# Attention scores: three rounded passes on the whole array, or plain float32 on its four quarters

## The chip, the cores and the metric

The kernel runs on one core of one Trainium2 chip. The metric is the device time of one execution in microseconds (us), lower is better. TensorE (PE in the profile) multiplies matrices: a stationary operand is loaded into its 128x128 array (PEld), a moving operand streams past it column by column, and the result goes to PSUM, which has eight banks. VectorE (DVE) and ScalarE (ACT) read PSUM; GpSimd (POOL) works on SBUF alone; SyncE (SP) issues the DMAs.

## The reference, cut to what matters

Block-causal attention over 4 x 8 heads of 576 tokens and 64 dimensions, then a squared-ReLU network over all 2304 tokens, then a top-1 mixture of eight experts. The change touches the first stage alone, and in it the scores:

```
scores = scale * matmul(q, k.T)                  # per head: 576 x 576, contraction over 64
scores = where(block_i >= block_j, scores, -1e9) # blocks of 64 tokens
attn = exp(scores - max) / sum
x = matmul(attn, v)
h = x @ w_in; g = s * relu(h)**2 + b; g @ w_out  # 512 -> 2048 -> 512
each token through one of 8 experts, 512 -> 1024 -> 512, chosen by an argmax over logits
```

The argmax over logits makes rounding matter: a token sent to another expert has another output row.

## The kernel before, in words

**Units and blocks.** Two heads of one batch make a unit; there are 16 units of 9 query blocks, so 144 steps. Block `i` of a unit needs the keys 0 to 64(i+1), which is `n` = 64 to 576 columns. Both heads are treated at once: the two transposed heads lie on partitions 0 to 63 and 64 to 127, and a stationary tile of queries is block diagonal (one head's queries in each corner, zeros elsewhere), so that one 128x128 product gives 64 query rows of either head, 128 rows in all.

**Scores (`scores`, L131 to L147).** TensorE multiplies rounded operands (fp32r) in one pass per column, at reduced precision; so queries and keys are split into a high, rounded part and a low rest, and a block takes three products: qh kh, qh kl, ql kh (L144), each over max(n, 256) columns. Blocks 0 and 1, which are narrower than 256, use plain float32 operands `qf`, `kf` (L141); a plain float32 product is two passes, and so stands in the profile as two matmuls. Block 8 has 576 columns and takes two PSUM banks of 288 each. The parts are made per unit by ACT (L104, L107: queries, scaled by 1/8; L119, L120, L128: keys) and DVE (`flush`: L88 and L90, the low parts).

**The rest of a step.** DVE takes the row maxima (L152), ACT the exponentials with their sums (L160), DVE the reciprocals (L177, L178), POOL scales the rows (L169), TensorE transposes them five steps later (L198, plain float32 transposes), ACT copies them out of PSUM (`p_copy`, L211), and `pv` (L227) multiplies them with the values: per head a product of 128 rows and 64 columns of the array in plain float32, the two heads on the two column halves of the array. Queries and keys of the next unit are transposed at blocks 4, 5 and 6 (L95, L125).

**PSUM banks.** The scores have three banks (`s`) in both stages: `BANKS_0 = (3, 3, 1, 1)` and `BANKS_A = (3, 2, 1)`. A bank comes free when the exponentials that read it are done.

**Order.** Up to step 45 (`ORDERED`), which is five units, the order on PE, ACT, DVE and POOL is the order in which the code emits. There the loop over `t` issues, in this order: transposes of step t-5, scores of t, exponentials of t-1, copies, reciprocals of t-2, maxima of t, low parts, a piece of weight conversion, and the next unit's transposes. From step 45 on a planner orders the instructions by the program's order and by its own estimates of when operands and banks are there, and from step 50 on it mixes in pieces of the squared-ReLU network (L470, L545), whose matmuls TensorE does beside attention. What of that network is left follows when attention has ended, near 326 us, and then come the experts. On every engine the instructions then run strictly in the planned order.

Of the kernel before, what the change touches and what calls it, by code (L numbers as in the profile page):

```python
# [9 lines left out]
F32 = mybir.dt.float32  # L10
F32R = mybir.dt.float32r
BF16 = mybir.dt.bfloat16
I32 = mybir.dt.int32
AF = mybir.ActivationFunctionType
ALU = mybir.AluOpType
AX = mybir.AxisListType
PSUM = bass.MemoryType.PSUM
P = 128


def attention(nc, tc, ctx, ps, ident, q, k, v, xT_d, weights):
# [7 lines left out]
    B, H, S, D = q.shape  # L29
    NB = S // D  # L30
    NU = B * H // 2
    pool = lambda n, b, **kw: ctx.enter_context(tc.tile_pool(name=n, bufs=b, **kw))
    fix = pool("a_fix", 1)
    raw = pool("a_raw", 2)
    vp = pool("a_v", 2)
    pt = pool("a_pt", PTBUF)
    kt = pool("a_kt", 2)
    pp = pool("a_p", NPBUF)
# [3 lines left out]
    one = fix.tile([P, 1], F32, name="one")  # L42
    nc.gpsimd.memset(one, 1.0)
    nc.scalar.activation(one, one, AF.Exp)
    qb, qf = [], []
    for par in range(2):
        qq = []
        for nm in ("qh", "ql"):
            t = fix.tile([P, NB - 2, 2, D], F32R, name=f"{nm}{par}")
            nc.gpsimd.memset(t.bitcast(F32), 0.0)  # L50
            qq.append(t)
        qb.append(qq)
        t = fix.tile([P, 2, 2, D], F32, name=f"qf{par}")
        nc.gpsimd.memset(t, 0.0)
        qf.append(t)
    st = {}
    todo = []
    scored = [None]
    copies, sums = [], []

# [17 lines left out]
            ps.last["load"] = nc.sync.dma_start(tail, src[b, h0:h0 + 2, 512:].rearrange("h p d -> p h d"))  # L78
            s["raw"].append(t)

    def low(scale, out, src, high):
        todo.append((scale, out, src, high))

    def flush():
        while todo:
            scale, o, src, high = todo.pop(0)
            if scale:
                nc.vector.scalar_tensor_tensor(o, src, 0.125, high.bitcast(F32), ALU.mult, ALU.subtract)  # L88
            else:
                nc.vector.tensor_sub(o, src, high.bitcast(F32))  # L90

    def transpose4(src):
        t = ps.t.tile([P, 512], F32, name="tw", tag="t")
        for c in range(4):
            nc.tensor.transpose(t[:, c * P:(c + 1) * P], src[:, c].rearrange("p h d -> p (h d)"), ident)  # L95
        return t

    def q_high(u, src, blocks):
        skip = max(2 - blocks.start, 0)
        for hh in range(2):  # L100
            r = slice(hh * D, hh * D + D)
            a = src[r].rearrange("p (i d) -> p i d", d=D)
            if skip:
                nc.scalar.activation(qf[u % 2][r, :, hh], a[:, 0:skip], AF.Copy, scale=0.125)  # L104
                a = a[:, skip:]
            oh, ol = (t[r, blocks.start + skip - 2:blocks.stop - 2, hh] for t in qb[u % 2])
            nc.scalar.activation(oh, a, AF.Copy, scale=0.125)  # L107
            low(True, ol, a, oh)

    def q_transpose(u):  # L110
        q_high(u, transpose4(st[u]["raw"][0]), slice(0, 8))

    def k_transpose(u):
        kh = kt.tile([P, S], F32R, name="kh", tag="kh")
        kl = kt.tile([P, S], F32R, name="kl", tag="kl")
        kf = kt.tile([P, P], F32, name="kf", tag="kf")
        st[u]["k"] = (kh, kl, kf)
        t = transpose4(st[u]["raw"][1])
        nc.scalar.copy(kf, t[:, 0:P])  # L119
        nc.scalar.copy(kh[:, 0:512], t)  # L120
        low(False, kl[:, 0:512], t, kh[:, 0:512])

    def tails(u):
        t = ps.t.tile([P, 512], F32, name="te", tag="t")
        nc.tensor.transpose(t[:, 0:P], st[u]["tail"].rearrange("p h d -> p (h d)"), ident)  # L125
        q_high(u, t[:, 0:D], slice(8, 9))
        kh, kl, _ = st[u]["k"]
        nc.scalar.copy(kh[:, 512:], t[:, D:2 * D])  # L128
        low(False, kl[:, 512:], t[:, D:2 * D], kh[:, 512:])

    def scores(u, i):  # L131
        kh, kl, kf = st[u]["k"]
        qh, ql = qb[u % 2]
        n = (i + 1) * D
        pr = pp.tile([P, 640], F32, name="p", tag="p")
        parts = [(0, n)] if i < 8 else [(0, 288), (288, 288)]
        scs = []
        for k0, w in parts:
            sc = ps.s.tile([P, 512], F32, name="sc", tag="s")
            if i < 2:  # L140
                scored[0] = nc.tensor.matmul(sc[:, 0:w], qf[u % 2][:, i].rearrange("p h d -> p (h d)"),  # L141
                                             kf[:, 0:w], start=True, stop=True)
            for j, (a, kk) in enumerate(((qh, kh), (qh, kl), (ql, kh)) if i >= 2 else ()):
                scored[0] = nc.tensor.matmul(sc[:, 0:max(w, 256)], a[:, i - 2].rearrange("p h d -> p (h d)"),  # L144
                                             kk[:, k0:k0 + max(w, 256)], start=(j == 0), stop=(j == 2))
            scs.append(sc)
        return u, i, pr, parts, scs  # L147

    def maxima(u, i, pr, parts, scs):
        nm = small.tile([P, 2], F32, name="nm", tag="nm")  # L150
# [30 lines left out]
    def p_transpose(u, blocks):  # L181
        i0 = blocks[0]
        grp = int(i0 >= 4)
        if i0 == 4 * grp:
            st[u]["pt", grp] = pt.tile(([P, 4, 2, P], [P, 5, 5, P])[grp], F32, name=f"pt{grp}", tag=f"pt{grp}")
        out = st[u]["pt", grp]
        nch = i0 // 2 + 1
        jobs = []
        if grp == 0:
            jobs.append(([(i, c) for i in blocks for c in range(nch)], out[:, i0:i0 + 2, 0:nch]))  # L190
        else:
            for c0, c1 in ((0, min(4, nch)), (4, nch)):
                if c1 > c0:
                    jobs.append(([(i0, c) for c in range(c0, c1)], out[:, i0 - 4, c0:c1]))
        for lst, o in jobs:
            t = ps.t.tile([P, 512], F32, name="tp", tag="t")
            for e, (i, c) in enumerate(lst):
                nc.tensor.transpose(t[:, e * P:(e + 1) * P], st[u][i][0][:, c * P:(c + 1) * P], ident)  # L198
            src = t[:, 0:len(lst) * P]
            if grp == 0:  # L200
                src = src.rearrange("p (i c n) -> p i c n", i=2, n=P)
            else:
                src = src.rearrange("p (c n) -> p c n", n=P)
            copies.append((i0, o, src))
        for i in blocks:
            st[u].pop(i)

    def p_copy():
        while copies:
            i0, o, src = copies.pop(0)  # L210
            P_COPY(nc, i0)(o, src)  # L211

    def pv(u, grp):

        s = st[u]
        if grp == 0:
            s["x"] = xo.tile([P, S], F32, name="x", tag="x")
        vt, p = s["raw"][2], s.pop(("pt", grp))
        n = 256 if grp == 0 else 320
        o = ps.o.tile([P, 512], F32, name="o", tag="o")  # L220
        cs = range(2) if grp == 0 else range(5)
        with tc.issue_after(scored[0].ins), tc.high_priority():
            for c in cs:
                first = max(0, 2 * c - 4 * grp)
                for hh in range(2):
                    r = slice(hh * D, hh * D + D)
                    nc.tensor.matmul(o[r, first * D:n], vt[:, c, hh], p[:, first:, c, r],  # L227
                                     start=(c == 0), stop=(c == cs[-1]))
        sums.append((u, grp, o, n))

    def x_copy():
# [14 lines left out]
    q_transpose(0)  # L246
    k_transpose(0)
    tails(0)
    flush()
    seq = [(u, i) for u in range(NU) for i in range(NB)]  # L250

    def at(t):
        return seq[t] if 0 <= t < len(seq) else (None, None)
# [24 lines left out]

    done = 0
    maxed = None  # L280
    order = ExitStack()
    order.enter_context(tc.manual_schedule(engines={mybir.EngineType.PE, mybir.EngineType.Activation,
                                                    mybir.EngineType.DVE, mybir.EngineType.Pool}))
    for t in range(len(seq) + LP + 1):
        if t == ORDERED:
            exponentials(*maxed)
            normalise(*at(t - 2))
            order.close()
        u, i = at(t - LP)
        if i in (3, 8):  # L290
            pv(u, int(i == 8))
            done += int(i == 8)
        if t < ORDERED:
            turn(t - LT)
            u, i = at(t)
            now = scores(u, i)
            if t >= 1:
                exponentials(*maxed)
            p_copy()
            x_copy()  # L300
            if t >= 2:
                normalise(*at(t - 2))
            maxed = maxima(*now)
            flush()
            weights(t)
            prepare(u, i)
            loads(u, i)
        else:
            x_copy()
            turn(t - LT)  # L310
            p_copy()
            u, i = at(t)
            if u is not None:
                exponentials(*maxima(*scores(u, i)))
                prepare(u, i)
                loads(u, i)
            u, i = at(t - LN)
            if u is not None:
                normalise(u, i)
            flush()  # L320
            weights(t)
        yield done

# [1160 lines left out]
```

## Time and profile before

| | |
|---|---|
| median of 3 runs | 904.42 us (903.22 to 905.1) |
| the profiled execution, its own time | 904.25 us |
| its span | 902.6 us |
| PE, PEld busy | 875.6 us (97%), 725.2 us (80%) |
| DVE, ACT, POOL busy | 642.5 us (71%), 568.4 us (63%), 215.1 us (24%) |

The page's strip of busy tenths in 40 slices of 22.6 us each:

```profile
PE   7999989999999999999999999999999999999996
PEld 5767777888879789999999999998477776776775
DVE  5898986464646355878967777767688987776783
ACT  6998786566757543333566655542288786776773
```

Matmuls are pipelined and their ends are modelled: a matmul's own duration (0.28 us for 256 columns) contains a latency that the next one hides, so what it costs TensorE is read from start to start. "Idle before" and the releaser behind it say what ended a wait. Line numbers (L144) are those of the kernel before.

### The profile page before, as it was taken

The numbers are of one execution on the slowest core, as the hardware profiler recorded it, in microseconds if no ns is written. First come the engines' busy times: TensorE is split into PE (matmuls) and PEld (weight loads), VectorE is DVE, ScalarE is ACT, GpSimd is POOL, SyncE is SP. The second block draws the span as 40 slices with busy tenths as digits, with TensorE's granted clock in tenths as the row PEclk, the third lists the DMA queues.
The fourth block names the chain that finished last, engine by engine and source line by source line (L and its number), as shares of the span: only waits on it lengthen the run. The fifth ranks groups of instructions, "written<-read, shape, count | busy, mean of one in ns | idle before, by whom it ended". The sixth has DMA issues, their size and how long they took to land. (4 is left out here: it accounts for less than half of the span.)

```text
span 902.6 us, 17057 instructions
## 1 busy us (share of the span) xinstructions
PE 875.6 (97%) x5765; PEld 725.2 (80%) x5765; DVE 642.5 (71%) x1490; ACT 568.4 (63%) x1165; POOL 215.1 (24%) x335
## 2 busy tenths in 40 slices
PE   7999989999999999999999999999999999999996
PEld 5767777888879789999999999998477776776775
DVE  5898986464646355878967777767688987776783
ACT  6998786566757543333566655542288786776773
POOL 5676564233333300000000000002034422222110
PEclk9999999999999999999999999999999999999999
DMA  6757433322321133445112222115346697637501
GB/s 161 199 149 189 140 108 79 101 53 77 77 73 28 61 113 106 148 141 184 48 49 69 70 61 58 48 48 180 124 148 232 234 384 250 222 131 252 196 13 39
DMA packets 109482, 113.84 MB, mean 126 GB/s; under 512 B 62680, under 2 KB 80618, under 8 KB 109388
## 3 DMA queue, kind: packets, MB, share of 16 engines
q1 hardware_dynamic: 105579, 100.74, 36.0%
q0 software_dynamic: 3808, 11.94, 3.8%
q8 instruction: 48, 0.79, 0.4%
q14 instruction: 47, 0.38, 0.1%
HBM read 143.58 MB, written 19.80 MB: 181 GB/s over the span
## 5 line engine op out<-in xcount | busy, mean ns | idle before, releaser
L470 PE MATMUL ph<-xh,wih 128*128 128x256 f32 x576 | 165.9, 288 | 0.0
L470 PE MATMUL ph<-xh,wil 128*128 128x256 f32 x576 | 162.7, 282 | 0.0
L470 PE MATMUL ph<-xl,wih 128*128 128x256 f32 x576 | 162.4, 282 | 0.0
L169 POOL TENSOR_TENSOR p<-p,rc 128x64 f32<-128x64 f32 (+2 forms) x144 | 108.3, 758 | 128.4 <-DVE rc L178 83.8
L470 PEld LDWEIGHTS ph<-xh,wih 128*128 128x128 f32 x576 | 109.2, 190 | 4.6 <-issue 2.9
L470 PEld LDWEIGHTS ph<-xl,wih 128*128 128x128 f32 x576 | 109.3, 190 | 1.3 <-issue 0.2
L470 PEld LDWEIGHTS ph<-xh,wil 128*128 128x128 f32 x576 | 109.3, 190 | 0.8 <-issue 0.6
L152 DVE TENSOR_REDUCE nm<-sc 128x1 f32<-128x288 f32 (+8 forms) x160 | 70.0, 447 | 44.2 <-PE sc L144 41.0
L160 ACT ACTIVATE p<-sc,nm 128x288 f32<-128x288 f32 (+8 forms) x160 | 81.2, 510 | 22.6 <-DVE rc L177 10.2
L1102 DVE TENSOR_TENSOR w1l<-raw,w1h 128x1024 fp32r<-128x1024 f32 x60 | 71.5, 1223 | 19.6 <-ACT w1h L1101 13.1
L1102 DVE TENSOR_TENSOR w2l<-raw,w2h 128x1024 fp32r<-128x1024 f32 x64 | 75.2, 1219 | 9.6 <-ACT w2h L1101 9.4
L1110 POOL DMA_INDIRECT xr<-x_d,gidx_e x2 | 2.3, 1130 | 310.2 <-PE ph L470 309.9
L198 PE MATMUL tp<-ident,p 128*128 128x128 f32 x400 | 65.8, 278 | 4.1 <-POOL p L169 1.7
L1101 ACT CAST w2h<-raw 128x1024 fp32r<-128x1024 f32 x64 | 65.8, 1053 | 5.1 <-PE py L1205 5.0
L480 ACT ACTIVATE r<-ph 128x512 f32<-128x512 f32 x44 | 26.3, 598 | 65.9 <-PE ph L470 65.8
L1101 ACT CAST w1h<-raw 128x1024 fp32r<-128x1024 f32 x60 | 61.4, 1050 | 7.4 <-PE ph L1188 6.2
L211 ACT COPY pt<-tp 128x512 f32<-128x512 f32 (+3 forms) x128 | 62.8, 508 | 4.2 <-PE tp L198 3.8
L481 DVE SCALAR_TENSOR_TENSOR r<-r,sc 128x512 f32<-128x512 f32 x44 | 36.3, 824 | 40.5 <-ACT r L480 40.1
L198 PEld LDWEIGHTS tp<-ident,p 128*128 128x128 f32 x400 | 46.2, 141 | 14.6 <-issue 4.0
L144 PE MATMUL sc<-kh,qh 128*128 128x256 f32 (+5 forms) x128 | 50.0, 391 | 2.6 <-ACT p L160 2.5
L1205 PE MATMUL py<-w2h,hh 128*128 128x512 f32 x128 | 51.5, 402 | 0.0
L227 PE MATMUL o<-pt,raw_v 128*64 128x320 f32 (+4 forms) x448 | 50.3, 364 | 0.6 <-ACT pt L211 0.4
(309 smaller groups left out, 2272.4 us busy)
## 6 DMA issues: line engine op xcount, KB each, us to landing
raw<-in_moe_w_dram SPq DMA_DIRECT2D x172, 512.0 KB
xr<-xT_d SPq DMA_DIRECT2D x19, 512.0 KB
wr<-in_moe_w_in_dram SPq DMA_DIRECT2D x16, 512.0 KB
wr<-in_moe_w_out_dram SPq DMA_DIRECT2D x16, 512.0 KB
row<-part_d SPq DMA_DIRECT2D x20, 256.0 KB
x_d<-row SPq DMA_DIRECT2D x18, 256.5 KB
xT_d<-x SPq DMA_DIRECT2D x16, 288.0 KB
raw_q<-in_q_dram SPq DMA_DIRECT2D x32, 128.0 KB
```

The lines of the kernel that those rows point to most:

```text
L144: scored[0] = nc.tensor.matmul(sc[:, 0:max(w, 256)], a[:, i - 2].rearrange("p h d -> p (h d)"), kk[:, k0:k0 + max(w, 256)], start=(j == 0) ...
L152: ps.last["max"] = nc.vector.tensor_reduce(nm[:, e:e + 1], scs[e][:, 0:w], AX.X, ALU.max, negate=True)
L160: ps.last["exp"] = nc.scalar.activation(pr[:, k0:k0 + w], scs[e][:, 0:w], AF.Exp, bias=nm[:, 0:1], accum_out=sm[:, e:e + 1])
L169: ps.last["scale"] = nc.gpsimd.tensor_mul(pr[:, 0:n], pr[:, 0:n], rc.to_broadcast([P, n]))
L198: nc.tensor.transpose(t[:, e * P:(e + 1) * P], st[u][i][0][:, c * P:(c + 1) * P], ident)
L211: P_COPY(nc, i0)(o, src)
L227: nc.tensor.matmul(o[r, first * D:n], vt[:, c, hh], p[:, first:, c, r], start=(c == 0), stop=(c == cs[-1]))
L470: nc.tensor.matmul(ph[:, e], self.wi[p][w][:, c, e * P:(e + 1) * P], x[a][:, c], start=(n == 0), stop=(n == 3 * KC - 1))
L481: nc.vector.scalar_tensor_tensor(r, r, self.sc[:, 0:1], r, ALU.mult, ALU.mult)
L1101: self.nc.scalar.copy(ws[0][c], r)
L1102: self.nc.vector.tensor_sub(ws[1][c], r, ws[0][c].bitcast(F32))
L1205: nc.tensor.matmul(py, hT[a][:, c], self.w2s[w][c // 2][:, c % 2 * D:c % 2 * D + D], start=(t == 0), stop=(t == 3 * KF - 1))
```

## The change

Queries and keys are kept as plain float32, one tile each per unit (`qt`, `kt`), without zeros. A block's score is two products, one per head, of 64 rows and 64 columns of the array: head 0 has rows 0 to 63, head 1 rows 64 to 127. Which column half a head's result goes to alternates with the block: an uncrossed block puts head 0 on the lower half of PSUM's partitions, a crossed one on the upper half. Two blocks in succession are emitted together, at even steps, and so name the four quarters of the array. The widths are exact (no padding to 256). Blocks 7 or 8 paired with another need three banks. Because in a crossed block the two heads have changed places, the copies out of the transposes (`swapped`, for blocks 4 and up) and the moving operand of the first `pv` group (`alternate`, for blocks 0 to 3) put them back through their access patterns. Banks, lags, the hand-written stage and everything behind attention stay as they are.

```diff
-    def low(scale, out, src, high):
-        todo.append((scale, out, src, high))
-    def flush():
...
-    def q_high(u, src, blocks):
...
+    def halves(u, nm, src, cols):
+        if nm not in st[u]:
+            st[u][nm] = kt.tile([P, S], F32, name=f"{nm}t", tag=f"{nm}t")
+        o = st[u][nm][:, cols]
+        if nm == "q":
+            nc.scalar.activation(o, src, AF.Copy, scale=0.125)
+        else:
+            nc.scalar.copy(o, src)
     def q_transpose(u):
-        q_high(u, transpose4(st[u]["raw"][0]), slice(0, 8))
+        halves(u, "q", transpose4(st[u]["raw"][0]), slice(0, 512))
...
+    def crossed(u, i):
+        return (u * NB + i) % 2
+    def scores(pair):
+        made, jobs = [], []
+        for u, i in pair:
+            n = (i + 1) * D
+            parts = [(0, n)] if i < 8 else [(0, 288), (288, 288)]
+            scs = [ps.s.tile([P, 512], F32, name="sc", tag="s") for _ in parts]
+            made.append((u, i, pp.tile([P, 640], F32, name="p", tag="p"), parts, scs))
+            jobs.append([*zip(parts, scs)])
+        for e in range(max(map(len, jobs))):
+            for (u, i), job in zip(pair, jobs):
+                if e >= len(job):
+                    continue
+                (k0, w), sc = job[e]
+                for hh in range(2):
+                    r = slice(hh * D, hh * D + D)
+                    o = slice(0, D) if hh == crossed(u, i) else slice(D, P)
+                    scored[0] = nc.tensor.matmul(sc[o, 0:w], st[u]["q"][r, i * D:i * D + D], st[u]["k"][r, k0:k0 + w],
+                                                 start=True, stop=True)
+        return made
...
+            elif crossed(u, i0):
+                src = src.rearrange("p (c h n) -> p c h n", h=2, n=D)
+                o = swapped(o.rearrange("p c (h n) -> p c h n", h=2))
...
+                    moving = alternate(p, first, c, (hh + crossed(u, 0)) % 2) if grp == 0 else p[:, first:, c, r]
...
-            now = scores(u, i)
+            if t % 2 == 0:
+                ready.extend(scores(seq[t:t + 2]))
+            now = ready.pop(0)
...
-            flush()
...
-                exponentials(*maxima(*scores(u, i)))
+                if t % 2 == 0:
+                    ready.extend(scores(seq[t:t + 2]))
+                exponentials(*maxima(*ready.pop(0)))
```

## Rows read from the trace of the kernel before

**Rows 1.** Windows by stage: length, then each engine's busy us, granted clock, DMA share, GB/s.

```profile
20.00:80.00 60.00, 54.64 (x398) 42.03 (x396) 52.92 (x184) 55.77 (x186) 42.08 (x77) 1.00 0.70 183
80.00:150.00 70.00, 65.64 (x479) 53.87 (x476) 58.91 (x161) 54.65 (x165) 44.03 (x69) 1.00 0.49 129
150.00:326.00 176.00, 174.21 (x1215) 146.46 (x1214) 91.54 (x282) 109.96 (x312) 52.01 (x110) 1.00 0.23 65
326.00:885.00 559.00, 557.01 (x3570) 463.49 (x3569) 422.28 (x822) 329.68 (x459) 65.49 (x54) 1.00 0.41 141
885.00:903.00 18.00, 10.54 (x51) 8.42 (x49) 6.01 (x6) 6.44 (x8) 1.95 (x2) 0.87 0.09 33
```

**Rows 2.** Timeline of PE, 45 to 49 us: start, duration, line, operands, shape, count, idle.

```profile
45.80 0.44 PE L141 MATMUL sc<-kf,qf 128*128 128x64 f32 x2 [0.51 <-ACT p L160]
46.27 0.87 PE L227 MATMUL o<-pt,raw_v 128*64 128x256 f32 x8
...
47.46 0.47 PE L141 MATMUL sc<-kf,qf 128*128 128x128 f32 x2
47.76 0.60 PE L198 MATMUL tp<-ident,p 128*128 128x128 f32 x4
48.12 0.36 PE L144 MATMUL sc<-kh,qh 128*128 128x256 f32 x1
48.32 0.28 PE L144 MATMUL sc<-kl,qh 128*128 128x256 f32 x1
48.44 0.28 PE L144 MATMUL sc<-kh,ql 128*128 128x256 f32 x1
48.56 0.60 PE L198 MATMUL tp<-ident,p 128*128 128x128 f32 x4
```

**Rows 3.** Timeline of PE around one product with the values, 117.6 to 121 us.

```profile
117.68 0.37 PE L144 MATMUL sc<-kl,qh 128*128 128x448 f32 x1
117.88 0.36 PE L144 MATMUL sc<-kh,ql 128*128 128x448 f32 x1
118.17 2.28 PE L227 MATMUL o<-pt,raw_v 128*64 128x320 f32 x20
120.38 0.66 PE L95 MATMUL tw<-ident,raw_q 128*128 128x128 f32 x4
```

**Rows 4.** Groups of ACT by line and shape, 20 to 80 us.

```profile
L107 ACT ACTIVATE qh<-tw 64x384 fp32r<-64x384 f32 x8 | 3.9, 493 | 0.0
L120 ACT CAST kh<-tw 128x512 fp32r<-128x512 f32 x4 | 2.4, 597 | 0.0
L104 ACT ACTIVATE qf<-tw 64x128 f32<-64x128 f32 x8 | 2.3, 291 | 0.0
L107 ACT ACTIVATE qh<-te 64x64 fp32r<-64x64 f32 x8 | 1.7, 218 | 0.1
L119 ACT COPY kf<-tw 128x128 f32<-128x128 f32 x4 | 1.0, 256 | 0.0
L128 ACT CAST kh<-te 128x64 fp32r<-128x64 f32 x4 | 0.9, 213 | 0.0
```

**Rows 5.** Groups of DVE by line and shape, 20 to 80 us.

```profile
L88 DVE SCALAR_TENSOR_TENSOR ql<-tw,qh 64x384 fp32r<-64x384 f32 x8 | 4.4, 549 | 0.1
L90 DVE TENSOR_TENSOR kl<-tw,kh 128x512 fp32r<-128x512 f32 x4 | 2.7, 681 | 0.0
L88 DVE SCALAR_TENSOR_TENSOR ql<-te,qh 64x64 fp32r<-64x64 f32 x8 | 1.7, 216 | 0.1
L90 DVE TENSOR_TENSOR kl<-te,kh 128x64 fp32r<-128x64 f32 x4 | 0.9, 224 | 0.1
```

**Rows 6.** Timeline of PE in the planned stage, 218 to 227 us.

```profile
218.07 0.45 PE L144 MATMUL sc<-kh,qh 128*128 128x448 f32 x1
...
218.77 0.40 PE L144 MATMUL sc<-kh,qh 128*128 128x512 f32 x1
...
226.96 0.49 PE L141 MATMUL sc<-kf,qf 128*128 128x128 f32 x2 [0.32 <-ACT p L160]
```

More of the change, by code (lines that the diff above doesn't have):

```diff
@@ L44, in attention @@
     nc.scalar.activation(one, one, AF.Exp)
[L45 to L55, printed above, removed]
     st = {}
-    todo = []
     scored = [None]
@@ L79, in load @@
             s["raw"].append(t)
-    def low(scale, out, src, high):
-        todo.append((scale, out, src, high))
-    def flush():
[L85 to L90, printed above, removed]
     def transpose4(src):
@@ L96, in transpose4 @@
         return t
-    def q_high(u, src, blocks):
[L99 to L108, printed above, removed]
+    def halves(u, nm, src, cols):
[6 more added lines that the diff above has]
+            nc.scalar.copy(o, src)
     def q_transpose(u):
-        q_high(u, transpose4(st[u]["raw"][0]), slice(0, 8))
+        halves(u, "q", transpose4(st[u]["raw"][0]), slice(0, 512))
     def k_transpose(u):
[L114 to L121, printed above, removed]
+        halves(u, "k", transpose4(st[u]["raw"][1]), slice(0, 512))
     def tails(u):
@@ L125, in tails @@
         nc.tensor.transpose(t[:, 0:P], st[u]["tail"].rearrange("p h d -> p (h d)"), ident)
[L126 to L147, printed above, removed]
+        halves(u, "q", t[:, 0:D], slice(512, S))
+        halves(u, "k", t[:, D:2 * D], slice(512, S))
+    def crossed(u, i):
[19 more added lines that the diff above has]
+        return made
     def maxima(u, i, pr, parts, scs):
@@ L211, in p_copy, with swapped, alternate @@
             P_COPY(nc, i0)(o, src)
+    def swapped(t):
+        a = t.ap if hasattr(t, "ap") else t[:].ap
+        (ps_, pn), (cs_, cn), (hs, hn), (ns, nn) = a
+        return bass.AP(t.tensor, t.offset + hs, [[ps_, pn], [cs_, cn], [-hs, hn], [ns, nn]])
+    def alternate(t, first, c, h):
+        t = t[:, first:, c]
+        (ps_, pn), (is_, in_), (ns, nn) = t.ap
+        return bass.AP(t.tensor, t.offset + h * D * ns, [[ps_, pn], [2 * is_, in_ // 2], [is_ + (D - 2 * h * D) * ns, 2], [ns, D]])
     def pv(u, grp):
@@ L226, in pv @@
                     r = slice(hh * D, hh * D + D)
-                    nc.tensor.matmul(o[r, first * D:n], vt[:, c, hh], p[:, first:, c, r],
-                                     start=(c == 0), stop=(c == cs[-1]))
+                    moving = alternate(p, first, c, (hh + crossed(u, 0)) % 2) if grp == 0 else p[:, first:, c, r]
+                    nc.tensor.matmul(o[r, first * D:n], vt[:, c, hh], moving, start=(c == 0), stop=(c == cs[-1]))
         sums.append((u, grp, o, n))
@@ L280, in attention @@
     maxed = None
+    ready = []
     order = ExitStack()
@@ L303, in attention @@
             maxed = maxima(*now)
-            flush()
             weights(t)
@@ L319, in attention @@
                 normalise(u, i)
-            flush()
             weights(t)
```

## The prediction, made before the changed kernel ran

> **What bounds the kernel now.** I read the stages first, since the busy shares of the whole span are a mean over stages with different limits. The windows [rows 1] show three kinds. From 20 to 80 us, the stage whose order is written by hand, no engine is alone at its limit: ACT is busy 55.77 of 60 us (93%), PE 54.64 (91%), DVE 52.92 (88%). From 80 to 150 us PE has 4.4 us of idle time in 70 and DVE is at 84%. From 150 to 885 us PE is busy 731.2 of 735 us and DVE and ACT have room; attention ends in it, near 326 us. So a microsecond that PE saves in the planned stage moves the end by about one, since PE has a full queue behind it up to 885; in the hand-written stage a saving counts only as far as all three engines get it.
>
> Then I priced the scores on PE from start to start. An fp32r pass of 256 columns takes 0.12 us (48.32 to 48.44), which is 0.47 ns a column, and the first pass behind plain float32 work takes 0.20 [rows 2]. A unit has 3 x (256 + 256 + 320 + 384 + 448 + 512 + 288 + 288) = 8256 such columns: 3.9 us. Eight first passes add 8 x 0.08 = 0.64; blocks 0 and 1 take 0.47 and 0.30 [rows 2]. Together 5.3 us a unit, 85 us over 16 units.
>
> **The price of the new products.** Rows 2 and 3 have plain float32. A full-array product of 128 columns takes 0.30 us from 47.46 to 47.76, less 0.08 for its first pass: 0.22 us for two passes, 1.7 ns a column [rows 2]. The product with the values has 3 x 320 + 192 + 64 = 1216 columns for each head, in 20 matmuls, and takes 2.21 us from 118.17 to 120.38 [rows 3]. At 1.7 ns a column one head alone needs 2.07 us, both in succession 4.1. So the two column halves do run at once. Of 2.21 us 0.14 is left for leaving the halves; entering them lengthens a 448-column pass from 0.20 us (117.68 to 117.88) to 0.29 (117.88 to 118.17) [rows 3]. A visit to the partitioned array thus costs about 0.2 us.
>
> No row has two row halves at work, so the quarters must be bounded. Best: all four at once. A pair then costs its wider block. Over two units, which hold nine pairs, that is 128 + 256 + 384 + 512 + 576 + 192 + 320 + 448 + 576 = 3392 columns x 1.7 ns = 5.8 us, 2.9 us a unit, and 4.5 visits x 0.2 = 0.9: 3.8 us, 1.5 less than now. Worst: nothing at once, 2 x 2880 columns x 1.7 = 9.8 us a unit and 0.9: 10.7, 5.4 more than now. I take four at once, by the nearest row, the column halves that run at full pace side by side. The Trainium skill (TensorE: Matmul & The Clock Gate, Part 3, "Measured speedup vs the span model") has a 4 x 4 packing by rows and columns at 10.6 times one tile's rate; it bears on the choice alone.
>
> **Whole and broken pairs.** A bank frees when its block's exponentials are done. There are three, a pair holds two, so the first block of the next pair can always start, and the second waits for the exponentials two blocks back (block 8's pairs for those one back as well). If PE fills that wait with other work, each block is a visit of its own: 2880 columns x 1.7 = 4.9 us and 9 x 0.2 = 1.8, 6.7 us a unit, 1.4 more than now. So a unit gains 1.5 us with whole pairs and loses 1.4 with broken ones: about half decides. In the planned stage the network's matmuls are the filler. For whole pairs speaks that blocks of 448 and 512 columns start 0.70 us apart in the plan of now (218.07, 218.77), with nothing else between; against it that a wait for ACT's release of a bank still occurs at 226.96 (0.32 us) [rows 6]. I take six whole pairs in ten: -0.6 x 1.5 + 0.4 x 1.4 = -0.34 us a unit; over the 99 planned steps, eleven units, -3.7 us.
>
> **The parts off TensorE.** ACT now spends 12.2 us on four units' parts of queries and keys, 3.05 a unit [rows 4]. It keeps two copies of 512 columns (0.597 each) and two tails (0.213): 1.62, so 1.4 less. DVE loses all its low parts, 9.7 us over four units, 2.4 a unit [rows 5]. In the hand-written stage, five units, the tightest engine is ACT. Its 1.4 us are the most I can count there; PE changes by -1.5 with whole pairs, and by +0.5 (4.9 + 0.9 against 5.3) where the second block of a pair waits alone, as the order by hand lets nothing between. Against the gain: a pair with block 8 waits for a third bank; behind it on PE stand the next transposes, and ACT's copies wait for those. The wait for a bank is 0.51 us now (45.80) [rows 2]; I take as much more per unit. Net -0.8 us a unit, -4 in all. From both sides: 5 x -1.5 = -7.5, and 0 if the waits eat it.
>
> In the planned stage ACT's and DVE's savings lie beside PE's work; of PE's 4.4 idle us from 80 to 150 [rows 1] I count 1 back. If that cover were gone the savings would not count against us, being savings. Edits that I price at nothing: `swapped` copies change only the order of 64-column runs, and stand beside PE's work; were each ACT copy as dear as its parts, ACT would lose what it gained in the hand-written stage (+4 on the sum). `alternate` reads runs of 64 as before. POOL's zeroing at the start lies beside the first loads. Block 0 of a unit is scored a step earlier, a step after its queries and keys are ready. No DMA moves on SP or POOL. The removed waits of PE for low parts were small; what is late next is the second bank.
>
> **Sum.** -3.7 - 4 - 1 = -8.7 us on the profiled execution's own 904.25 us (0.2 below the median of 904.42): 895.5 us. With the shares of whole pairs from 40% to 80% and the hand-written stage from 0 to -7.5 this case's own range is 886 to 903.
>
> **Rivals.**
> *Everything whole.* The planner is backlogged, every bank is free when a pair's turn comes: 11 x -1.5 = -16.5, -6.5 by hand, -1: 880 us. For it: PE's full queue from 150 us on [rows 1]. Against it: three banks for nine pairs of which two need all three.
> *The odd bank runs ahead (slower).* The third bank lets the first block of the next pair go alone each time, and the planner puts network matmuls before the second. All broken: 11 x 1.4 = +15.4, -2 by hand: about 918 us. It decides from two broken pairs in three: 11 x (-1.5 + 2.9 b) = 5, the other gains, gives b = 0.68. For it: the wait at 226.96 [rows 6] and the steady 80 to 150 us, where attention runs ahead of the network; against it the back-to-back blocks at 218 [rows 6].
> *Halves of one block take turns.* Both heads of a block write one bank, from different row halves. If those cannot, a pair costs twice its wider block: 2 x 2.9 + 0.9 = 6.7 us a unit, +1.4, with about -2 by hand: 918 too, and that with whole pairs; with a share broken up to 925. In the trace two column halves write one bank at full pace [rows 3], which speaks against it; nothing shows it for row halves. The Trainium skill (TensorEngine Tiling, "Restrictions and Gotchas", Gotcha 1) says that different row tiles cannot use one PSUM bank at the same time; by that rule the time is this rival's, by the row on column halves my own. No run here shows it yet.
> *The change does not do what it says:* no quarter beside another, 16 x 5.4 = +86 us, 990. *The clock falls:* PE's granted clock is 1.00 of its 2.4 GHz level through 885 us and 0.87 only at the end, where PE is busy 10.5 of 18 us [rows 1]. If a hand-written stage of small products let it fall to 1.2 GHz, PE's 54.64 us there would near double: up to +45.
>
> **Chances and range.** My forecast 0.50, all whole 0.12, odd bank 0.13, halves in turn 0.13, no concurrency or a fallen clock 0.06, savings that cancel to nothing 0.06. The range 880 to 921 holds some 8 in 10: it leaves out the last two on the far side and the far part of halves in turn. A difference under 0.2% (1.8 us) cannot be told from none. Faster: 0.46 of the 0.50, and 0.12: 0.58. Same: 0.03 and 0.06: 0.09. Slower: the rest, 0.33.
>
> **What would show it.** Matmuls of a pair should start in fours within some 0.03 us, and a pair of 448 and 512 columns take about 0.9 us from start to start; twice that means halves in turn, four times no concurrency. Whole against broken pairs is read from what stands between the two blocks on PE in 150 to 326 us. ACT and DVE should show 1.4 and 2.4 us less a unit, the hand-written stage should end some 4 us earlier, and waits of scores for ACT's exponentials should grow around blocks 7 and 8. The prediction fails if these waits grow by over 1 us a unit, if most pairs are broken, or if the row halves don't run at once.

## The result, and the profile after

The changed kernel takes 915.47 us (median of 4 runs, 914.72 to 916.85) against 903.82 us for the kernel before on the same chip: a ratio of 1.0128, 95% interval 1.0113 to 1.0143. It is slower by 11.7 us where 8.7 us less was forecast. The profiled execution took 914.72 us, its span is 913.1 us.

Windows of the changed kernel by stage, in the columns of [rows 1]:

```profile
20.00:80.00 60.00, 54.11 (x435) 30.00 (x433) 44.74 (x154) 50.10 (x159) 41.14 (x73) 1.00 0.70 184
80.00:150.00 70.00, 69.20 (x506) 43.31 (x505) 46.23 (x140) 49.61 (x148) 45.55 (x72) 1.00 0.49 129
150.00:326.00 176.00, 173.34 (x1232) 124.36 (x1231) 72.52 (x241) 98.91 (x271) 50.57 (x109) 1.00 0.21 58
326.00:885.00 559.00, 556.94 (x3603) 463.72 (x3602) 418.37 (x819) 328.24 (x459) 65.79 (x54) 1.00 0.42 143
885.00:914.00 29.00, 20.94 (x100) 17.06 (x98) 12.43 (x13) 12.42 (x17) 3.10 (x3) 0.93 0.08 30
```

The savings off TensorE are there: in the first stage ACT has 5.7 us less to do than in [rows 1] and DVE 8.2 us less. The granted clock is 1.00 through 885 us. But from 80 to 150 us PE has lost its idle time (69.20 of 70 us busy, 65.64 before). The stage that had room is full, and its time has not become shorter.

Two measures of progress are worked out from the traces. The first is when the exponentials of a step end (steps counted from 0, nine a unit). The change is ahead by 2.2 us at step 18 and by 0.5 at step 42, behind by 1.0 at step 48 and by 9.8 at the last (324.8 against 315.0 us). So the hand-written stage is no longer the matter by its end, and the planned stage loses the time. The second is PE's time from each matmul's start to the next one's, put down to the earlier of the two, from step 42 to the end of attention; idle are the gaps of over 0.15 us between the end of one matmul and the start of the next:

| us on PE | before | after |
|---|---|---|
| scores | 57.7 | 59.1 |
| transposes of weights (`tp`) | 28.4 | 35.9 |
| transposes of queries and keys (`tw`, `te`) | 9.0 | 11.6 |
| network, second product (`pxa`) | 51.6 | 52.9 |
| network, first product (`ph`) | 55.6 | 55.6 |
| idle | 7.5 | 5.0 |
| product with the values (`o`) | 33.9 | 33.9 |
| all | 243.7 | 254.1 |

The scores' own row hardly grows; the transposes' rows grow by 10.1 us, and the reason lies at the border between a transpose and the scores behind it. In the kernel before, the first rounded pass of 256 columns takes 0.20 us instead of 0.12, but the transpose ahead of it lasts only 0.028 us to the next start instead of 0.109 (four of them take 0.36 us in [rows 2], from 47.76 to 48.12). Together they cost what they cost apart: the 0.08 us are moved from one row to the other, 59 times in this stretch. In the changed kernel the transpose ahead of the scores lasts 0.203 us.

**The quarters do run at once.** PE's timeline of the changed kernel in the hand-written stage, in the columns of [rows 2]; x8 is two blocks, two heads and two passes, all printed under the width of the first:

```profile
60.80 0.71 PE L171 MATMUL tp<-ident,p 128*128 128x128 f32 x5
61.44 0.66 PE L118 MATMUL sc<-kt,qt 64*64 64x192 f32 x8
62.03 1.20 PE L171 MATMUL tp<-ident,p 128*128 128x128 f32 x9
63.16 0.88 PE L118 MATMUL sc<-kt,qt 64*64 64x320 f32 x8
63.97 0.44 PE L72 MATMUL tw<-ident,raw_q 128*128 128x128 f32 x2
```

The pair of 192 and 256 columns takes 0.59 us from start to start (61.44 to 62.03), that of 320 and 384 0.81 (63.16 to 63.97). 128 columns more on the wider block cost 0.22 us: 1.7 ns a column, the price forecast for four at once. The first passes of the four products start within 0.02 us of each other (61.439 to 61.459), though the heads of one block write one bank from different row halves. Beyond its columns a visit costs 0.59 - 256 x 1.7 ns = 0.155 us, and the matmul ahead of it, a transpose, lasts 0.203 us to the next start where inside its own row it lasts 0.109: 0.25 us a visit in all, charged in part to the transposes.

**Visits that are broken.** The same view of the handover and of the planned stage; x2 is the two passes of one head alone:

```profile
77.14 0.80 PE L118 MATMUL sc<-kt,qt 64*64 64x256 f32 x6
77.87 0.66 PE L171 MATMUL tp<-ident,p 128*128 128x128 f32 x4
78.54 0.85 PE L118 MATMUL sc<-kt,qt 64*64 64x384 f32 x2
79.32 0.33 PE L171 MATMUL tp<-ident,p 128*128 128x128 f32 x1
79.58 0.85 PE L118 MATMUL sc<-kt,qt 64*64 64x384 f32 x2
...
267.87 0.86 PE L118 MATMUL sc<-kt,qt 64*64 64x384 f32 x2
268.65 0.66 PE L72 MATMUL tw<-ident,raw_q 128*128 128x128 f32 x4
269.24 0.98 PE L118 MATMUL sc<-kt,qt 64*64 64x384 f32 x6
```

From 78.54 to 80.37 one block of 384 columns is scored, one head at a time with a transpose between: three quarters of the array stand still, and 1.83 us go, with the transpose, where a whole pair does this block and one of 320 beside it in 0.81. From 75 us on there are 76 visits for 49 pairs; 27 pairs are whole, and 15 visits hold one head alone.

**Waits in the hand-written stage.** The same view there:

```profile
27.51 0.27 PE L93 MATMUL te<-ident,raw_t 128*128 128x128 f32 x1
27.71 1.07 PE L118 MATMUL sc<-kt,qt 64*64 64x512 f32 x8
29.32 0.70 PE L118 MATMUL sc<-kt,qt 64*64 64x288 f32 x4 [0.53 <-ACT p L133]
29.95 0.98 PE L171 MATMUL tp<-ident,p 128*128 128x128 f32 x7
30.86 0.33 PE L118 MATMUL sc<-kt,qt 64*64 64x64 f32 x4
31.78 0.43 PE L118 MATMUL sc<-kt,qt 64*64 64x128 f32 x4 [0.58 <-ACT p L133]
32.14 0.87 PE L216 MATMUL o<-pt,raw_v 128*64 128x256 f32 x8
```

The pair of blocks 7 and 8 takes 2.24 us (27.71 to 29.95) where its columns and a visit make 1.13; the pair behind it 1.28 where they make 0.37. The printed idle (0.53, 0.58) is only part of such a wait, since a matmul's own duration covers the rest.

The groups that answer to [rows 4], ACT from 20 to 80 us; DVE has none left of [rows 5]:

```profile
L81 ACT ACTIVATE qt<-tw 128x512 f32<-128x512 f32 x4 | 2.8, 688 | 0.0
L83 ACT COPY kt<-tw 128x512 f32<-128x512 f32 x4 | 2.3, 581 | 0.0
L81 ACT ACTIVATE qt<-te 128x64 f32<-128x64 f32 x4 | 0.9, 233 | 1.2 <-PE te L93 1.2
L83 ACT COPY kt<-te 128x64 f32<-128x64 f32 x4 | 0.9, 218 | 0.0
```

### The profile page after: what moved, and what is told of

The parts are those of the page before. It is cut to its first block, busy times and chain, and to the rows that moved or that the text cites. A ratio compares the mean times of both kernels' runs of the same rounds, so it can differ in the third digit from the quotient of the medians.

```text
span 913.1 us, 17227 instructions
## 1 busy us (share of the span) xinstructions
PE 888.6 (97%) x5957; PEld 685.7 (75%) x5957; DVE 602.1 (66%) x1394; ACT 550.2 (60%) x1085; POOL 213.1 (23%) x329
## 5 line engine op out<-in xcount | busy, mean ns | idle before, releaser
L118 PE MATMUL sc<-kt,qt 64*64 64x288 f32 (+8 forms) x640 | 90.4, 436 | 8.0 <-ACT p L133 7.2
L471 DVE SCALAR_TENSOR_TENSOR r<-r,sc 128x512 f32<-128x512 f32 x44 | 33.9, 770 | 50.6 <-ACT r L470 50.4
L171 PE MATMUL tp<-ident,p 128*128 128x128 f32 x400 | 61.6, 280 | 0.7 <-ACT pt L187 0.7
L171 PEld LDWEIGHTS tp<-ident,p 128*128 128x128 f32 x400 | 44.5, 141 | 22.3 <-issue 8.8
L118 PEld LDWEIGHTS sc<-kt,qt 64*64 64x64 f32 x640 | 26.7, 134 | 34.2 <-ACT p L133 17.7
```

Of the source, the lines that this page charges most:

```text
L118: scored[0] = nc.tensor.matmul(sc[o, 0:w], st[u]["q"][r, i * D:i * D + D], st[u]["k"][r, k0:k0 + w], start=True, stop=True)
L471: nc.vector.scalar_tensor_tensor(r, r, self.sc[:, 0:1], r, ALU.mult, ALU.mult)
```

## The experiments

The theory: the planner puts other matmuls between the products of a pair, and each interruption costs a visit's price and the columns that then run alone. The rivals: visits cost more than was reckoned even when whole; or the banks hold the pairs up. Each ratio below is to the kernel before on the same chip at the same time (903.9 to 905.6 us).

**Glue the products of a pair (planned stage only).**

```diff
+        with ExitStack() as glue:
+            if late and lead:
+                glue.enter_context(tc.issue_after(lead[0].ins))
+                glue.enter_context(tc.high_priority())
             scored[0] = nc.tensor.matmul(...)
+        lead.append(scored[0])
```

> Changed kernel, but in the planned stage the matmuls of a pair after the first one are queued behind the first and have priority over all else that is ready. Its order on TensorE has 68 visits to the quarters in the planned stage (77 in the changed kernel) and none with a head alone (28). Theory 'broken pairs' (the 10 us were lost where the planner put other matmuls between the matmuls of a pair): at 1.7 ns a column and 0.2 us a visit the scores of the planned stage need 48.8 us, not 58.5, so 915.5 - 9.7 = about 906 us. Rival 'the quarters are dear in themselves, by waits of DVE and ACT for them': within 2 us of 915.5.

Measured: 907.21 us, ratio 1.0023 (1.0013 to 1.0032), about what the theory expected; 67 visits, none with one head alone. PE's timeline of this kernel at the place shown above:

```profile
78.36 0.66 PE L177 MATMUL tp<-ident,p 128*128 128x128 f32 x4
79.02 0.86 PE L123 MATMUL sc<-kt,qt 64*64 64x384 f32 x4
79.81 0.33 PE L177 MATMUL tp<-ident,p 128*128 128x128 f32 x1
79.89 0.36 PE L466 MATMUL ph<-xh,wih 128*128 128x256 f32 x1
80.19 0.97 PE L123 MATMUL sc<-kt,qt 64*64 64x448 f32 x4
```

The two heads of a block now stand together (x4), and the block takes 0.79 us, without the second visit of 0.79 and the transpose between. This edit alone, which changes only the planner's order, takes back most of the loss: the ratio falls from 1.0128 to 1.0023. That is the order's part, shown. Pairs can still part between their blocks.

**Hold the first product back until the second block's bank is free.**

```diff
+   if late and not lead:
+       glue.enter_context(behind(exps[-1 if any(b == 8 for _, b in pair) else -2]))
```

> As the first, and the first matmul of a pair waits for the exponentials that free the second block's bank (with block 8 in the pair: those one block later). The order has 54 visits, nearly all of whole pairs. Theory 'broken pairs': 40.7 us of scores in the planned stage, 915.5 - 17.8 = about 898 us, under the kernel before. Rival 'waits': holding the first block back makes maxima and exponentials later still, so not under 913 us, rather above 915.

Measured: 907.46 us, ratio 1.0024 (1.0014 to 1.0033). The visits fell to 53 and scores on PE to about what was expected, but not the time: missed. PE waits here as in the next experiment, where the rows are shown (for banks 5.4 us in 11 waits from 80 to 326 us, 2.2 in the changed kernel).

**The same order in the plan alone, without the wait on the chip.**

```diff
-   mybir.DependencyInfo(mybir.DependencyClass.Sync, ...)
+   mybir.DependencyInfo(mybir.DependencyClass.Sync, mybir.DependencyReason.SCHED_ONLY)
...
-       glue.enter_context(behind(exps[-1 if any(b == 8 for _, b in pair) else -2]))
+       glue.enter_context(behind(exps[-1]))
```

> As the second experiment, but the first matmul of a pair is tied to the exponentials of the block right before the pair in the plan alone: the plan places the pair later, and the chip waits for nothing but the banks. 50 visits, 39.5 us of scores. In the second run PE's scores fell to 40 us as expected, but PE waited some 10 us for ACT's and POOL's releases from 80 to 326 us, where the changed kernel waits 3.3. Theory 'the plan counts on releases earlier than they come': with the margin these waits fall back to 3 to 5 us and the time to 900 to 903 us, with the kernel before at about 904.5. Rival 'the waits come with whole pairs, wherever they are put': 907 again.

Measured: 904.39 us, ratio 1.0009 (0.9999 to 1.0018): missed by little, and level with the kernel before. 49 visits for 49 pairs; from step 42 on the scores take 40.4 us of PE instead of 57.7 before. PE's waits from 80 to 326 us (total, times, longest), first of the changed kernel, then of this one:

```profile
PE sc L118 <- ACT p L133: 2.2, 5, 0.8
PE tp L171 <- ACT pt L187: 0.7, 1, 0.7
```

```profile
PE sc L136 <- ACT p L152: 5.5, 9, 1.3
PE tp L191 <- ACT pt L207: 1.7, 5, 0.8
...
PE tp L191 <- POOL p L161: 0.8, 1, 0.8
PE tp L191 <- POOL p L162: 0.7, 2, 0.4
```

All pairs are whole, and the 17.3 us saved on scores are given back: transposes of weights +5.3, of queries and keys +1.5, the network's first product +6.2, its second +1.2, idle +4.6, values +0.3: 19.1. The transposes' share is no wait but the border of a visit: the 59 short transposes of the kernel before are gone (4.75 us), and the entry into the quarters lengthens the matmul ahead of a visit. Ten more network matmuls inside the stretch are 1.2 us. The rest is waits, those above and, as far as the trace tells, short ones within a matmul's duration. On this kernel a score no longer goes when its own bank is free, but when two or three are, and PE stands behind it.

**Break the pairs more: each score with high priority on its own.**

```diff
-   ready.extend(scores(seq[t:t + 2]))
+   with tc.high_priority():
+       ready.extend(scores(seq[t:t + 2]))
```

> Changed kernel, but in the planned stage all matmuls of the scores have priority over everything else that is ready, each for itself, with nothing that holds a pair together. The order breaks more pairs: 105 visits, 33 of them with a head alone, and it puts scores between the matmuls with the values. Theory 'broken pairs': 73.4 us of scores in place of 58.5, +15, about 930 us, and some more for the broken products with the values. Rival 'waits': earlier scores help maxima and exponentials, so 915 or less.

Measured: 949.11 us, ratio 1.0494 (1.0475 to 1.0512): the direction expected and more of it. 104 visits, 26 with one head alone, and the product with the values is cut up too. Its timeline shows scores alternating with single matmuls of the network:

```profile
119.91 0.49 PE L536 MATMUL pxa<-woh,gl 128*128 128x512 f32 x1
120.33 0.43 PE L118 MATMUL sc<-kt,qt 64*64 64x128 f32 x4
120.70 0.50 PE L536 MATMUL pxa<-woh,gh 128*128 128x512 f32 x1
121.12 0.66 PE L118 MATMUL sc<-kt,qt 64*64 64x192 f32 x8
```

**No pairs at all: each block scored by itself, in both stages.**

```diff
-   if t % 2 == 0:
-       ready.extend(scores(seq[t:t + 2]))
+   if True:
+       ready.extend(scores(seq[t:t + 1]))
```

> Changed kernel without pairs: each block's two products are emitted at its own step, so at most two of the four quarters work at once; everything else is as in the changed kernel. The order has 98 visits in the planned stage and 10 with a head alone: 72.4 us of scores against 58.5, +14; in the hand-written stage a unit's scores take 6.7 us of TensorE in place of 3.8 but that engine is not alone at its limit there: 0 to +8. Theory 'broken pairs': 929 to 937 us. Rival 'pairing costs more than it gives' (three banks for two blocks): below 915 us.

Measured: 928.6 us, ratio 1.0258 (1.0241 to 1.0275), at the lower edge of what was expected. 98 visits; attention ends 23.8 us later than before, and 3.2 of these stand at step 42 already. With the others it gives a row of ratios: 49 visits 1.0009, 53 1.0024, 67 1.0023, 76 1.0128, 98 1.0258, 104 1.0494. The order of visits and the order of ratios agree but for the two that are level; it is no law, since the last kernel cuts up other products too.

**The new products in the hand-written stage alone (units 0 to 4).**

```diff
+NEW = 5
...
+            if not new(u):
+                now = scores(u, i)     # three rounded passes, as before
+            else:
+                if t % 2 == 0:
+                    ready.extend(scores2([x for x in seq[t:t + 2] if new(x[0])]))
+                now = ready.pop(0)
```

> The change in the hand-written stage alone (units 0 to 4, block 8 of unit 4 without a partner); units 5 to 15 as before. Theory 'the change gains 1 to 2 us by step 40 and gives them back before the planned stage': ratio to the kernel before 0.998 to 1.001. Rival, the prediction's term for this stage, -4 us: 0.9955. Second rival, the loss is made here: over 1.004.

Measured: 902.67 us, ratio 0.9996 (0.9987 to 1.0005): a hit. Step 42 ends 0.2 us later than before, step 48 at the same time, the last 0.1 later. So the hand-written stage gives nothing to the total, though ACT and DVE do less in it.

**The rounded passes, but without DVE's low parts (the second and third product take the high parts).**

```diff
     def low(scale, out, src, high):
-        todo.append((scale, out, src, high))
+        pass
```

> The kernel before without the low parts on DVE; its second and third products take the high parts again, so TensorE and ACT do the same work (the scores are less exact). Theory 'in the hand-written stage ACT or the chain from scores to maxima to exponentials is the limit, not DVE's 2.4 us a unit': ratio 0.997 to 1.000. Rival 'the low parts stand in the way of the maxima': -1.5 us or more a unit by hand, 0.992 or less.

Measured: 921.72 us, ratio 1.0201 (1.0187 to 1.0215), which can't be read for the question: other tokens go to other experts, and each of the three products of the experts' second layer has 136 matmuls instead of 128. The attention can be read, and there the expectation missed: step 42 ends 3.6 us earlier (0.7 us a unit), step 78 9.0, the last 6.8. DVE's low parts did stand partly on the path in the kernel before. The change takes the same work away and is 0.5 us ahead at step 42, so something else holds it up.

**A fourth bank for the scores in the hand-written stage (the weight conversion does without its bank).**

```diff
-BANKS_0 = (3, 3, 1, 1)
+BANKS_0 = (4, 3, 1)
...
-    converted[0] = conv.send((CONV[step], banks.f if step < ORDERED else None))
+    converted[0] = conv.send((CONV[step], None))
```

> Changed kernel with a fourth bank for scores in the hand-written stage; for it the weight conversion there loses its PSUM bank and works in SBUF (DVE has room: 44.7 of 60 us). The planned stage has three as before. Theory 'pairs with block 8 wait for the third bank, that is what eats the hand-written stage's gain': PE's 5.0 us of waits for exponentials in the first 80 us fall under 2, step 44 comes 2 to 4 us earlier, about 912 us against 915.5. Rival 'the gain is lost elsewhere': 915 or more.

Measured: 915.48 us (4 runs), ratio 1.0132 (1.0117 to 1.0148): the time missed. The profiled execution took 911.8 us, as expected; the other three took 915.4 to 916.3 at a lower mean granted clock (0.994 to 0.995 against 0.997), so the median doesn't show what the bank alone is worth. The place itself is clear. PE's timeline of this kernel at the pair of blocks 7 and 8:

```profile
27.13 1.32 PE L118 MATMUL sc<-kt,qt 64*64 64x512 f32 x12
28.38 0.98 PE L171 MATMUL tp<-ident,p 128*128 128x128 f32 x7
```

The twelve matmuls now stand in one row and take 1.25 us, against 2.24 with three banks. Step 42 ends 2.9 us earlier than before (0.5 in the changed kernel). At step 48 it is 0.2 us late again. So the lack of a fourth bank is what holds the hand-written stage up, and what a fourth one gives is mostly lost at the handover; at the last step 2.3 us of it are left (7.55 us late, 9.83 in the changed kernel).

**Both: whole pairs in the plan and four banks by hand.**

```diff
 # on top of the kernel with the order in the plan alone
-BANKS_0 = (3, 3, 1, 1)
+BANKS_0 = (4, 3, 1)
```

> The fifth and the eighth experiment together: pairs kept whole by the plan in the planned stage, and the fourth bank for scores in the hand-written stage. Theory 'the two parts add': the fifth run was at 1.001 of the kernel before; the eighth came to step 48 2 us earlier than the changed kernel: ratio 0.998 to 0.999, about 902.5 us where the kernel before is at 904. Rival 'what is won by hand is lost in the planned stage's waits': 1.000 to 1.002.

Measured: 904.75 us, ratio 1.0003 (0.9993 to 1.0013): missed; the second of the two accounts fits. Step 42 ends 2.8 us earlier than before, step 48 1.3 later. PE's timeline of this kernel at the handover:

```profile
72.98 1.09 PE L191 MATMUL tp<-ident,p 128*128 128x128 f32 x8
76.37 0.38 PE L480 MATMUL ph<-xh,wih 128*128 128x256 f32 x1 [2.30 <-ACT xh L392]
```

PE reaches the network's first matmul sooner, and waits 2.30 us there for its operand. ACT, which makes it, has itself waited for a load:

```profile
75.27 1.04 ACT L392 CAST xh<-xr 128x1024 fp32r<-128x1024 f32 x1 [2.19 <-DMA xr<-xT_d]
```

So the lead of the hand-written stage runs into the load of the network's input. It is issued at 71.47 us, 1.7 us sooner than in the kernel before (73.19), which is less than the lead of 2.8.

**More of the network's pieces due beside attention.**

```diff
-PIECE_D = 2.8
+PIECE_D = 2.4
```

> As the ninth, with the network's pieces emitted every 2.4 steps instead of 2.8, so that TensorE has more other work between the pairs. In the fifth run PE is idle 11 us from 80 to 326 us (6.2 in the kernel before), much of it 0.7 to 1.1 us at a time ahead of pairs that come behind block 8. Theory 'filler is lacking': 3 to 5 us less than the ninth. Rival 'the order is fixed by the plan and the wait for a bank comes at its place whatever is left over': within 1.5 us of the ninth.

Measured: 915.74 us, ratio 1.0122 (1.0108 to 1.0136): missed by a wide margin. Attention ends 15.0 us later than before, and the pieces run out of operands behind it. PE's longest wait after 326 us, and the window behind it:

```profile
PE ph L480 <- ACT xh L392: 10.1, 1, 10.1
```

```profile
343.50:357.00 13.50, 5.57 (x24) 5.27 (x25) 3.73 (x5) 1.84 (x3) 0.00 (x0) 0.50 0.61 199
```

The granted clock is 0.50 there, the 1.2 GHz level. The later end of attention is mostly network work done sooner: its two products take 128.2 us of PE from step 42 to the end of attention, 114.6 in the ninth run. What the run loses on the ninth, 11.0 us, is about the wait and the stretch at the lower clock behind it. So it settles nothing on how much filler the stage wants.

**Transposes and values one step later, with one buffer of weights more.**

```diff
-LAGS = (1, 5, 7)
-NPBUF = 6
+LAGS = (1, 6, 8)
+NPBUF = 7
```

> As the ninth, with the transposes six steps behind the scores instead of five, the products with the values eight instead of seven, and a seventh buffer for the probabilities. PE's waits for POOL's scaling and ACT's copies were 3.2 us from 80 to 326 us in the fifth run and 2.4 us for POOL by hand in the eighth. Theory 'transposes come too early': these fall under 1 us and the time by 2 to 4 us from the ninth. Rival: the waits only move to the banks, within 1.5 us.

Measured: 906.09 us, ratio 1.0023 (1.0013 to 1.0032): missed. The hand-written stage becomes worse (step 42 ends 2.1 us later than before, step 48 6.2), the planned stage takes some of it back (the last step 3.0).

No version is faster than the kernel before by more than can be measured.

## Why the prediction was wrong

**What bounds the kernel: right.** PE has a full queue from 80 us to the end, and what attention loses by its end (9.8 us) comes out in the total (10.5 between the two profiled executions, 11.7 between the medians).

**Four quarters at once at 1.7 ns a column: right.** With that the rival by which halves of one block take turns falls. The Trainium skill (TensorEngine Tiling (Array Packing), "Restrictions and Gotchas", Gotcha 1) says that different row tiles cannot use one PSUM bank at the same time. The trace does not agree: both heads of a block write one bank in 0.81 us where turns would need 1.3 us for the columns alone (2 x 384 x 1.7 ns). The measurement decides, for this case. The clock did not fall.

**Parts off TensorE: the engine time right.** The four copies a unit are 1.72 us (688 + 581 + 233 + 218 ns) where 1.62 was forecast; DVE's low parts are gone.

**"Six of ten pairs whole, -3.7 us": the step that failed, mostly in its prices.** The share was nearly right, 27 of 49. At the prices forecast that is 0.55 x 3.8 + 0.45 x 6.7 = 5.1 us a unit. The trace has, over 11 units, 43.6 us of columns (counted with everything of one visit at once), 76 visits x 0.25 = 19.0, and 4 us of waits within visits: 66.6 us, 6.05 a unit, 0.75 more than the 5.3 reckoned for the kernel before. And the 5.3 are too many. They hold 0.64 us for eight first passes, which the transposes ahead give back. Counted in the same way, with what the matmuls ahead of a visit lose or gain, the scores of the kernel before take 57.7 - 3.6 = 54.1 us, 4.9 a unit. So the change costs 12.5 us there instead of saving 3.7, and 2.5 of them come back as less idle time. The differences to the forecast 5.0:

- a visit costs 0.25 us, not 0.2: +0.3 a unit. The price was read from the switch to two column halves [rows 3] and rounded down from 0.14 + 0.09; leaving four quarters takes 0.155, and entering 0.094;
- columns are 4.0 us a unit, not 3.7, because breaks go through blocks as well: the prediction knew whole pairs and single blocks, not a single head with three quarters idle;
- waits for banks within a visit, 0.35 a unit, were counted only in the hand-written stage;
- 6.9 visits a unit, not 6.3: +0.1.

To these comes the price of the kernel before, 4.9 instead of 5.3: another 0.4 a unit.

With these prices a whole pair's unit is 2.9 + 4.5 x 0.25 = 4.0 and a broken one's 4.9 + 9 x 0.25 = 7.15, and against 4.9 the line from which the change gains lies at about 70% of whole pairs before any wait, not near half. The forecast, six in ten, stood on the wrong side of it. That the order is at fault and not the products is shown by the glue, which left the products alone and took back most of the loss.

**"-4 us by hand": failed, mis-sized in one term.** The wait for a third bank was put at 0.51 us more a unit, after one wait of [rows 2]. From 20 to 75 us PE spends 21.4 us in 19 visits, for 11.3 us of columns and 19 x 0.155 = 2.9 of leaving: 7.2 us of waits over nearly four units, 1.8 a unit, against about 1.0 reckoned in all. With the entries (19 x 0.094) that is 5.9 us a unit on PE, so nothing is left there of the 1.5 that whole pairs were to save: in the kernel before the visits of this stretch take 25.9 us over four units, waits within them included, and 28 transposes ahead are 2.3 us shorter in all, 5.9 a unit too. The fourth bank shows that the wait is the cause: 2.9 us ahead at step 42, against 0.5. What is ahead there is then lost at the handover, 1.5 us in the changed kernel and 4.1 with four banks and whole pairs; in the latter the wait behind a load takes 2.30 us of it.

**"Everything whole, 880 us": its saving came true in part, its time did not.** With the order in the plan alone the scores fell by 17.3 us in the planned stage; with the borders of the visits counted, from 54.1 to 44.5 us: 9.6 where 11 x 1.5 = 16.5 had been reckoned. And the kernel was only level. The rival counted the bank as free when a pair's turn comes; it isn't (waits for banks 5.5 us from 80 to 326 us, 2.2 in the changed kernel), and PE, which runs in order, waits with all its filler behind it.

**The rival "the odd bank runs ahead", 918 us, came nearest**, with that of the halves in turn, but not by its mechanism: it wants two pairs in three broken, and the trace has less than half.

**The sum's own range was added up wrongly.** By its terms 40% of whole pairs and nothing by hand give 0.24 x 11 - 1 = +1.6 us, an upper end of 906 and not 903.

**Open.** How much of what whole pairs give back belongs to the three banks, and how much to the planner's estimates of when they come free. A fourth bank in the planned stage would tell; all eight banks are in use there, and it wasn't tried. The two runs on filler and lags did not settle it.

## What to carry to other kernels

A product that is cheap only beside its neighbours needs an order that keeps them together: price the visit (here 0.25 us), count the visits that the order on record really has, and glue the group before judging the product. Price it together with the matmul ahead of it, in both kernels: what a first pass seems to cost can be time that its neighbour has saved. A group that needs several buffers at once starts when the last of them is free: count buffers against groups, not against blocks, and add what stands behind the group on an engine that runs in order. Where an engine's saving is the argument, look at which wait ends last in that stage, and at the place where the stage hands over; here 8.2 us less on DVE and 5.7 less on ACT gave nothing.

## What the runs showed of the hardware

Two row halves of TensorE write one PSUM bank at the same time here, where they write different partitions: the first passes of a pair start 7 ns apart (61.439, 61.446, 61.453, 61.459 us), and four plain float32 products of 64 rows and 64 columns run at the pace of one, 1.7 ns a column. No run shows it for rounded operands.

A transpose ahead of a rounded pass lasts 0.028 us to the next start instead of 0.109, and the pass 0.20 instead of 0.12; ahead of the quarters the transpose lasts 0.203.

The granted clock fell to 1.2 GHz beside attention or right behind it in four of the experiments. It did so for 3.4 us at 78.3 us where four banks and whole pairs had left PE busy 4.29 of the 8.30 us before. It did so again around the wait of 10.1 us shown above, which lasts from 340.8 to 351.0 us: the clock is down from 343.5 to 357.2, and a matmul of the network then takes 0.21 us from start to start instead of 0.12. A wait on PE can thus cost more than its length. The changed kernel has no such fall through 885 us.
